# Seven products for eight of the sixteen expert tiles in six token-block pairs of a Fourier-mixing and expert-retrieval kernel, with operand sums formed on GpSimd

## The chip, the cores and the metric

The kernel runs on one core of a Trainium2 chip. The metric is the device time of one execution in microseconds (us). A core has five engines that run their own instruction streams in order and wait for each other by semaphores: TensorE (PE in the profile, with PEld for its weight loads), VectorE (DVE), ScalarE (ACT), GpSimd (POOL) and SyncE (SP), which issues the transfers here.

## What is computed

The input is 2048 tokens of 512 numbers, normalised first (`xn`). The result is the sum of three: the input, a Fourier mixing of `xn` by DFT matrices, and a retrieval of experts. The last takes nearly all the time:

```python
def _B_ref(x, w_q, k1, k2, u, v):            # H = 32 heads, E = 64, N = 4096 experts, K = 2
    q = jnp.einsum("nd,dhc->nhc", xf, w_q)
    s1 = jnp.einsum("nhd,ed->nhe", q[..., :dk], k1)
    s2 = jnp.einsum("nhd,ed->nhe", q[..., dk:], k2)
    ...
    top_s = jnp.take_along_axis(cand, ord2, axis=-1)
    top_e = jnp.take_along_axis(eidx, ord2, axis=-1)
    g = _softmax(top_s, axis=-1)
    ue = u[top_e]
    ve = v[top_e]
    act = _gelu(jnp.einsum("nd,nhkd->nhk", xf, ue))
    return jnp.einsum("nhk,nhk,nhkd->nd", g, act, ve)
```

Each token scores 64 + 64 half keys in each of 32 heads, keeps the two best of their sums, and adds up two experts of 4096 a head, weighted.

## The kernel before

**Numbers in two halves.** A float32 operand is kept as two float16 arrays, `h` (the rounded value) and `l` (the rest). A product is three matmuls, (h,h), (h,l) and (l,h), accumulated in PSUM. The split of a raw array is an ACT copy to `h` and a GpSimd subtraction for `l`.

**The scores.** The 32 heads are eight chunks j, the tokens 16 blocks i of 128. For each (j, i), 128 in all, `scores` (with `s_mm`) runs 12 matmuls of 512 columns (L247) into one of four PSUM banks, ACT evicts it (L891), and DVE finds the best values and their places (MAX8 L895, FIND_INDEX8 L899). M(j), the weights of a chunk, are products of the query weights and the keys: raw weights are split by ACT and GpSimd (`m_prep`; GpSimd's are L161 and L162) during the chunk before, and multiplied on PE (`m_mul`, L143) at fixed places amid the scores of that chunk, after i = 3, 4, 5 and 7. Routing of chunk j-1 (`routing`) is done by GpSimd and DVE in turns during chunk j, after i = 1, 2 and 4; the values to be combined pass between the two engines (L824 to L864). L535 and L536 fold rows of the Fourier part.

**Weights of the experts.** The 4096 experts are 16 tiles of 256, each two chunks of 128. `u` and `v` are loaded in float32, scaled and split by `fill_uv` and `stage_v` (ACT L774, L775 and L789; GpSimd L776 and L791) in slots of the table `todo`, a list of functions for each (j, i). `u` stays in SBUF; seven tiles of `v` go to the scratch `v_d` in DRAM. The list `fills` gives the order, u first for tiles 0 to 3, 8 to 14.

**The expert stage.** Instead of gathering, the kernel computes all activations of all experts and multiplies them with a sparse weight matrix. Phase z of a pair of token blocks (b, b+1) multiplies the two x blocks with all 32 chunks of u: `u_part` runs 12 matmuls of 256 columns for each chunk (L1027; two chunks to a bank), and ACT applies the gelu (L1034). Single blocks, 0, 1, 14 and 15, run with 128 columns. Then come two v phases, in which 96 matmuls of 512 columns (L1110) form the output of a block, and DVE and SP add and store it. In between the gates are built: one-hot matrices by DVE (L1055, L1060, L1063), multiplied on PE with 32 columns (L1065), and combined with the activations by DVE and ACT (L1073 to L1081). The order of phases is z0, z1, v0, then z(b,b+1), v(b-1), v(b) for b = 2, 4 to 12, then z14, v13, z15, v14, v15. Checks of the inputs' form run beside it (transfers named `cx` and `fit`), and if one fails, a slower version (`safe`) does the work again.

**What sets the order.** The program is written in a loop order with the tables `todo` and `plan`; a scheduler then arranges the instructions on each engine, which runs them in that order. A tile that is written again waits for all earlier readers, a store among them.

## Time and profile before

| | |
|---|---|
| median of 3 runs | 1146.23 us (1145.19 to 1146.46) |
| the profiled execution | 1147.81 us |
| its span | 1146.0 us |
| mean granted clock of TensorE | 0.996 |
| transfers over the span | 142.69 MB read, 17.63 MB written |

The span lies inside the execution's time. A window row names a stretch of the span and gives the time for which each engine was busy in it, with the count of its instructions in brackets, then the granted clock, the share of the 16 DMA engines, and GB/s. A group row names line, engine, operation and tiles, then a count; behind the bar it has the busy time, the mean of one in ns, and the idle time of the engine just before, with what ended it. A timeline row has the start, the duration and the line, and in brackets the idle time before it with the releaser. A piece of the chain of waits has a start, a duration and a count of instructions.

### The profile page before, as it was taken

To read this page: it belongs to the slowest core of one execution; us is meant where nothing else is said; L and a number is where in the kernel's file an instruction comes from. 1 tells how busy PE (TensorE), PEld (TensorE's weight loads), DVE (VectorE), ACT (ScalarE), POOL (GpSimd) and SP (SyncE) were. 2 spreads that over 40 slices of the span, in tenths; PEclk is the share of its full clock that TensorE was granted. 3 is DMA by queue.
4 is the path that set the end of the run, shared out by engine and by line. 5 is a ranking of instruction groups with operands and counts; after the bars stand their busy time and mean duration, and the time that the engine had idled before them with its cause. 6 is when DMAs were issued, how large, how long until landed. Compare 5 with 4: busy or idle time off the path is not lost.

```text
span 1146.0 us, 25270 instructions
## 1 busy us (share of the span) xinstructions
PE 1134.4 (99%) x9884; PEld 726.5 (63%) x9884; DVE 929.8 (81%) x2819; ACT 600.7 (52%) x1047; POOL 247.2 (22%) x265
## 2 busy tenths in 40 slices
PE   9999999999999999999999999999999999999997
PEld 6455454544544469687488478479569569658763
DVE  7899959899899999956985895896896796888570
ACT  6557487677686554353445445435526536433440
POOL 1415296675674400000000000000010010000000
PEclk8999999999999999999999999999999999999999
DMA  8884435234232104352742742742644545451422
GB/s 285 273 217 155 164 122 178 98 125 148 93 111 79 52 15 142 113 172 86 240 165 77 255 157 88 237 165 101 215 161 147 179 166 170 157 174 68 130 74 105
DMA packets 98335, 167.82 MB, mean 146 GB/s; under 512 B 32916, under 2 KB 48155, under 8 KB 98206
## 3 DMA queue, kind: packets, MB, share of 16 engines
q1 hardware_dynamic: 97904, 166.04, 43.1%
q8 instruction: 79, 1.29, 0.4%
q14 instruction: 50, 0.41, 0.1%
q10 hardware_dynamic: 302, 0.08, 0.0%
HBM read 142.69 MB, written 17.63 MB: 140 GB/s over the span
## 4 chain that ended last, share of the span: by engine, by line
PE 78%; DVE 12%; POOL 4%; DMA 2%; ACT 1%; issue 1%; SPq 0%; DVEq 0%; POOLq 0%; ACTq 0%
PE v L1110 28%; PE z L1027 27%; PE s L247 16%; PE g L1065 4%; DVE vals L895 3%; DVE idx L899 2%; PE m L143 1%; PE m L147 1%; DVE u L895 1%; POOL w L161 1%; DVE L L1055 1%; PE p L444 1%; DVE u L899 1%; DMA u<-in_vn_dram 1%; DVE act L1081 1%
## 5 line engine op out<-in xcount | busy, mean ns | idle before, releaser
L1027 PE MATMUL z<-xb,u 128*128 128x256 f16 (+1 forms) x3840 | 342.8, 251 | 0.1
L1027 PEld LDWEIGHTS <-u 128*128 128x128 f16 x3840 | 309.8, 98 | 26.5 <-issue 0.2
L247 PE MATMUL s<-m,xq 128*128 128x512 f16 x1344 | 297.2, 379 | 0.0
L1110 PE MATMUL v<-v,act 128*128 128x512 f16 x1056 | 233.2, 379 | 0.0
L247 PEld LDWEIGHTS <-xq 128*128 128x128 f16 x1344 | 129.7, 98 | 150.9 <-issue 1.0
L1055 DVE TENSOR_TENSOR L<-io_lam,cmp 128x2048 f16<-128x2048 f16 x128 | 156.1, 1220 | 60.4 <-PE g L1065 60.2
L1110 PEld LDWEIGHTS <-act 128*128 128x128 f16 x1056 | 101.4, 98 | 117.6
L1123 POOL TENSOR_TENSOR y<-y,xr 128x512 f32<-128x512 f32 x15 | 27.9, 1859 | 610.0 <-DMA y<-y_d 410.7
L895 DVE MAX8 vals<-ss 128x8 f32<-128x64 f32 x896 | 133.7, 216 | 6.3 <-ACT ss L891 6.2
L1034 ACT ACTIVATE act<-z,scl 128x256 f32<-128x256 f32 (+1 forms) x152 | 72.6, 502 | 121.7 <-PE z L1027 121.7
L1110 PE MATMUL v<-v,w 128*128 128x512 f16 x480 | 106.2, 379 | 0.0
L1186 ACT ACTIVATE cx<-cx 128x896 f32<-128x896 f32 x64 | 60.5, 945 | 69.7 <-DVE cx L1166 51.9
L891 ACT ACTIVATE ss<-s,wsc 128x512 f32<-128x512 f32 x120 | 79.4, 681 | 32.6 <-PE s L247 17.4
L899 DVE FIND_INDEX8 idx<-vals,ss 128x8 uint16<-128x256 f32 x224 | 93.9, 419 | 0.0
L1080 ACT ACTIVATE act<-w 128x1024 f16<-128x1024 f32 x36 | 48.4, 1360 | 62.6 <-DVE w L1073 62.1
L1110 PEld LDWEIGHTS <-w 128*128 128x128 f16 x480 | 46.1, 98 | 53.4
L1073 DVE SCALAR_TENSOR_TENSOR w<-act,scl,g 128x1024 f32<-128x1024 f32 x44 | 55.7, 1276 | 19.8 <-ACT act L1034 19.8
L1160 DVE TENSOR_TENSOR cx<-cx 128x512 f32<-128x512 f32 (+2 forms) x84 | 48.5, 612 | 26.8 <-DMA cx<-in_cb_dram 23.8
L1065 PEld LDWEIGHTS <-L 128*128 128x128 f16 x2048 | 60.7, 96 | 11.8 <-issue 1.3
L1081 DVE TENSOR_TENSOR act<-w,act 128x1024 f16<-128x1024 f32 x44 | 60.2, 1371 | 3.7 <-ACT act L1080 3.7
L1065 PE MATMUL g<-R,L 128*128 128x32 f16 x2048 | 61.9, 176 | 0.8 <-DVE R L1063 0.7
L1063 DVE TENSOR_TENSOR R<-R,cmp 128x512 f16<-128x512 f16 x128 | 60.8, 475 | 1.5
(320 smaller groups left out, 1318.5 us busy)
## 6 DMA issues: line engine op xcount, KB each, us to landing
v<-v_d SPq DMA_DIRECT2D x67, 512.0 KB, 4.1
cx<-in_cb_dram SPq DMA_DIRECT2D x64, 448.0 KB, 4.4
w<-in_wq_dram SPq DMA_DIRECT2D x28, 512.0 KB, 6.0
fit<-in_wq_dram SPq DMA_DIRECT2D x28, 512.0 KB, 5.0
uv<-in_vn_dram SPq DMA_DIRECT2D x16, 512.0 KB, 4.1
uv<-in_ut_dram SPq DMA_DIRECT2D x16, 512.0 KB, 5.7
c<-in_ca_dram SPq DMA_DIRECT2D x8, 512.0 KB, 7.2
y<-y_d SPq DMA_DIRECT2D x16, 256.0 KB, 3.6
```

The lines of the kernel that those rows point to most:

```text
L247: nc.tensor.matmul(ps, xt[i][:, l, kd, :], m[:, r, kd, :], start=(n == 0), stop=(n == 3 * KD - 1))
L891: nc.scalar.activation(s, ps, AF.Copy, scale=inv)
L895: nc.vector.max(vals[:, i, w, :, h], s[:, g, :])
L899: nc.vector.max_index(idx[:, i, w].rearrange("p k h -> p (k h)"), vals[:, i, w, 0:2].rearrange("p k h -> p (k h)"), s[:, w * HC:g + 1, :]. ...
L1027: nc.tensor.matmul(ps if n == 1 else ps.rearrange("p (b n) -> p b n", b=2), ug[:, l, c % 2, kd, :], xb2[:, k0, r, kd, :] if n == 1 else xb ...
L1034: nc.scalar.activation(ACT[bb][:, cg * m:cg * m + m, :], pv[:, i], AF.Gelu_apprx_tanh, scale=zsc)
L1055: nc.vector.tensor_tensor(L.rearrange("p t (l two) -> p t l two", two=2), io_lam.rearrange("p (l two) -> p l two", two=2).unsqueeze(1).to_ ...
L1063: nc.vector.tensor_tensor(Rv, Rv, bc(2, NC), op=ALU.mult)
L1065: nc.tensor.matmul(p[:, hf, t * NC:(t + 1) * NC], L[:, t, :], R[:, t, :], start=True, stop=True)
L1081: nc.vector.tensor_tensor(w16[..., 1], w, w16[..., 0], op=ALU.subtract)
L1110: nc.tensor.matmul(pv, w16[:, c, :, l], v_sb[g][:, r, cc, :], start=(n + cc == 0 and k == 0), stop=(n == 15 and cc == 1 and k == 2))
L1186: later.append(lambda: nc.scalar.activation(tf[:, P:], tf[:, P:], AF.Abs, accum_out=chk[:, n:n + 1]))
```

## The change

For the six pairs b = 2, 4 to 12, the eight tiles of the two quads (0 to 3) and (8 to 11) are multiplied in Winograd's form of Strassen's scheme: the two chunks of a tile, the two halves of the 512 long contraction and the two token blocks make a 2x2 by 2x2 block product, done with seven block products and additions. The other eight tiles, `PLAIN`, stay as they were.

- **Sums of u.** `sum_u` forms four sums of quarter tiles by GpSimd (L808 to L811 of the changed kernel), `split4` splits them (ACT L794, GpSimd L795) and stores both halves, 256 KB each, to the scratch `s_d`. It hangs behind `fill_uv` of the eight tiles.
- **Sums of x.** `sum_x` adds the halves of x (L821), forms four sums (L826 to L829), splits, and stores to `t_d`, once a pair, written at slots 62 + 7n. Both use the space of the v tiles 5 to 8 as scratch, which is filled later.
- **The products.** `z_pair` runs the products of both quads with the plain groups between them in the order of `SEQ`; `slot` is one product of 24 matmuls of 128 columns (L1153). Its weights are u itself or a tile of sums from a ring of three places (`ring_load`, L1136), its moving operand x or `x4`, the sums of the pair. A quad is three PSUM banks, X, Y and Z, that take several products each; ACT copies them out, DVE adds three times, and four gelus of 128x512 take the place of eight of 128x256.
- **PSUM.** Four banks `z0` to `z3` go round by a list (`take`, `banks`) in the expert stage; before, two tags had two buffers each.

```diff
+QUADS = (0, 1, 2, 3), (8, 9, 10, 11)
+PAIRS = tuple(range(2, 14, 2))
...
             nc.gpsimd.tensor_tensor(dl, raw, dh, op=ALU.subtract)
+            if which == 0 and not safe and any(g in q for q in QUADS):
+                SRAW[g] = raw
+                sum_u(g, 0)
+
+        def scratch(g):
+            return v_sb[g].rearrange("p l c d -> p (l c d)").bitcast(F32)
+
+        def split4(part, t, h, dst):
+
+            l = t.bitcast(F16)[:, 0:2 * D]
+            if part == 0:
+                nc.scalar.activation(h, t, AF.Copy)
+                nc.gpsimd.tensor_tensor(l, t, h, op=ALU.subtract)
+                return
+            for i, v in enumerate((h, l)):
+                nc.sync.dma_start(dst(i), v)
+
+        def sum_u(g, part):
+
+            qd, t = next((n, q.index(g)) for n, q in enumerate(QUADS) if g in q)
+            s4 = scratch(8)
+            if part == 0:
+                raw = SRAW.pop(g)
+                a = [raw[:, c, k * 256:k * 256 + 256] for c in range(2) for k in range(2)]
+                r = [s4[:, k * 256:k * 256 + 256] for k in range(4)]
+                nc.gpsimd.tensor_tensor(r[0], a[2], a[3], op=ALU.add)
+                nc.gpsimd.tensor_tensor(r[1], r[0], a[0], op=ALU.subtract)
+                nc.gpsimd.tensor_tensor(r[2], a[0], a[2], op=ALU.subtract)
+                nc.gpsimd.tensor_tensor(r[3], a[1], r[1], op=ALU.subtract)
+                return
+            split4(part - 1, s4, v_sb[6].rearrange("p l c d -> p (l c d)")[:, 0:2 * D],
+                   lambda i: s_d[qd].rearrange("o p (t l f) -> t l p o f", t=4, l=2)[t, i])
+
+        def sum_x(b, part):
+
+            f, t4 = scratch(5), scratch(7)
+            if part == 0:
+                v = xq[b // 2]
+                nc.gpsimd.tensor_tensor(f.rearrange("p (q f) -> p q f", q=2),
+                                        v[:, :, 0].rearrange("p q k n -> p q (k n)"),
+                                        v[:, :, 1].rearrange("p q k n -> p q (k n)"), op=ALU.add)
...
+                nc.gpsimd.tensor_tensor(r[0], b12, b11, op=ALU.subtract)
+                nc.gpsimd.tensor_tensor(r[1], b22, r[0], op=ALU.subtract)
+                nc.gpsimd.tensor_tensor(r[2], b22, b12, op=ALU.subtract)
+                nc.gpsimd.tensor_tensor(r[3], b21, r[1], op=ALU.subtract)
+                return
+            split4(part - 1, t4, v_sb[6].rearrange("p l c d -> p (l c d)")[:, 2 * D:],
+                   lambda i: t_d[b // 2, :, i * 2 * D:i * 2 * D + 2 * D])
...
+            if which == 0 and not safe and any(g in q for q in QUADS):
+                todo[n + 1].append(lambda at, g=g: (sum_u(g, 1), sum_u(g, 2)))
+        if not safe:
+            for n, b in enumerate(PAIRS):
+                for part, at in enumerate((0, 2, 3)):
+                    todo[62 + 7 * n + at].append(lambda at, b=b, part=part: sum_x(b, part))
...
-            p = (pc if (n == 2 or b == (0,)) and cg % 4 > 1 else pb)(f"z{b[0]}_{cg}")
+            p, tag = take(f"z{b[0]}_{cg}")
+            banks.append(tag)
...
+            SEQ = ["c", "1a", "2a", "5a", "c", "6a", "3a", "c", "7a", "c", "4a", "1b", "2b", "5b", "c", "6b", "3b", "c",
+                   "7b", "c", "4b", "c"]
...
+        def ring_load(at):
+            for p, (qd, o) in PENDING.pop(at, ()):
+                t = RING[qd, o] = sx.tile([P, 4, 2, 2, P], F16, tag=f"s{p}", name=f"s{qd}_{o}_{at}")
+                nc.sync.dma_start(t.rearrange("p t l k e -> p (t l k e)"), s_d[qd, o])
...
+        def slot(op, quad, bank, qd):
+
+            ua, us, ub, xa = OPS[op]
+            for t, g in enumerate(quad):
+                k = 0
+                for kd in range(2):
+                    for l, r in ((0, 0), (0, 1), (1, 0)):
+                        if us is None:
+                            lt = u_sb[g][:, l, ua // 2, ua % 2 * 2 + kd, :]
+                        else:
+                            lt = RING[qd, us][:, t, l, kd, :]
+                        rt = xb2[:, (0, 0, 1, 1)[xa], r, xa % 2 * 2 + kd, :] if ub is None else x4[:, r, ub, kd, :]
+                        nc.tensor.matmul(bank[:, t * P:(t + 1) * P], lt, rt, start=(t == k == 0 and op in "125"),
+                                         stop=(t == 3 and k == 5), skip_group_check=op not in "125")
+                        k += 1
+            if us is not None:
+                ring_load(used[0])
+                used[0] += 1
...
+                    if op == "1":
+                        nc.scalar.activation(dst(0, 0), v(X), AF.Copy)
+                    elif op == "2":
+                        nc.vector.tensor_tensor(dst(0, 0), v(Y), dst(0, 0), op=ALU.add)
+                        banks.append(Yt)
+                    elif op == "5":
+                        nc.scalar.activation(dst(1, 0), v(Z), AF.Copy)
+                    elif op == "6":
+                        nc.scalar.activation(dst(0, 1), v(X), AF.Copy)
+                        gelu(dst(0, 0))
+                    elif op == "3":
+                        nc.vector.tensor_tensor(dst(0, 1), v(Z), dst(0, 1), op=ALU.add)
+                        banks.append(Zt)
+                    elif op == "7":
+                        nc.scalar.activation(dst(1, 1), v(X), AF.Copy)
+                        nc.vector.tensor_tensor(dst(1, 1), dst(1, 1), dst(1, 0), op=ALU.add)
+                        gelu(dst(0, 1))
+                    else:
+                        gelu(dst(1, 0), v(X))
+                        gelu(dst(1, 1))
+                        banks.append(Xt)
```

The lines of the changed kernel are numbered later: L535, L536 become L540, L541; L161, L162 become L166, L167; L776 and L791 become L782 and L849; L824 becomes L882.

**GpSimd at the end of chunk j=0 and in the first third of j=1**, up to the first row of routing. Here `u` in the folds are buffers of the Fourier part. Before:

```order
L535 TENSOR_TENSOR u_126<-u_126 128x127
L535 TENSOR_TENSOR u_126<-u_126 128x128
L536 TENSOR_TENSOR u_126<-u_126 128x127
L536 TENSOR_TENSOR u_126<-u_126 128x128
L824 TENSOR_TENSOR c_0_1304<-u_132 128x64
```

Now (v_920 and v_922 are the scratch of the sums, v_921 their upper halves, xq_108 the x of a pair):

```order
L795 TENSOR_TENSOR v_922<-v_922,v_921 128x1024
L828 TENSOR_TENSOR v_922<-v_920 128x256
L540 TENSOR_TENSOR u_128<-u_128 128x127
L540 TENSOR_TENSOR u_128<-u_128 128x128
L541 TENSOR_TENSOR u_128<-u_128 128x127
L541 TENSOR_TENSOR u_128<-u_128 128x128
L826 TENSOR_TENSOR v_922<-v_920 128x256
L827 TENSOR_TENSOR v_922<-v_920,v_922 128x256
L829 TENSOR_TENSOR v_922<-v_920,v_922 128x256
L821 TENSOR_TENSOR v_920<-xq_108 128x1024
L882 TENSOR_TENSOR c_0_1306<-u_134 128x64
```

The third pair's subtraction, the fourth pair's operations and the addition for the fifth now stand ahead of routing of j=0, behind the work for the first and second. The six sums of x as a whole moved to j=0 and j=1, and three subtractions L795 of theirs stand between this routing and the next weights' first split. L826 writes the place that the store behind L795 reads.

**GpSimd in chunk j=3**, from a split of an expert tile to the first row of routing (`w` are the next chunk's weights). Before:

```order
L776 TENSOR_TENSOR u_128<-uv_3_2341,u_128 128x1024
L161 TENSOR_SCALAR w_124<-w_124,wsc 128x1024
L162 TENSOR_TENSOR w_124<-w_124,wh_0_2477 128x1024
L776 TENSOR_TENSOR u_133<-uv_8_2418,u_133 128x1024
L161 TENSOR_SCALAR w_124<-w_124,wsc 128x1024
L162 TENSOR_TENSOR w_124<-w_124,wh_1_2536 128x1024
L824 TENSOR_TENSOR c_0_2622<-vals_1927 128x64
```

Now, from the first of those weights on:

```order
L166 TENSOR_SCALAR w_126<-w_126,wsc 128x1024
L167 TENSOR_TENSOR w_126<-w_126,wh_0_2507 128x1024
L795 TENSOR_TENSOR v_923<-v_923,v_921 128x1024
L782 TENSOR_TENSOR u_135<-uv_8_2444,u_135 128x1024
L810 TENSOR_TENSOR v_923<-uv_8_2444 128x256
L808 TENSOR_TENSOR v_923<-uv_8_2444 128x256
L809 TENSOR_TENSOR v_923<-v_923,uv_8_2444 128x256
L811 TENSOR_TENSOR v_923<-uv_8_2444,v_923 128x256
L166 TENSOR_SCALAR w_126<-w_126,wsc 128x1024
L167 TENSOR_TENSOR w_126<-w_126,wh_1_2574 128x1024
L795 TENSOR_TENSOR v_923<-v_923,v_921 128x1024
L882 TENSOR_TENSOR c_0_2664<-vals_1941 128x64
```

Two sums of four operations and a subtraction (of the tiles 3 and 8; the four operations of tile 3 stand just ahead of these rows) now lie between that split and routing. The same happens with the tiles 0 and 1 in j=2 and with 9, 10 and 11 in j=4.

**SP in the z phase of the pair (4, 5)**, the transfers of the checks and the ring. Before:

```order
L875 DMA_TRANSPOSE zt_9807<-z_d 128x3x128
L1122 DMA xr_9046<-in_x_dram 128x512
L1139 DMA cx_8199<-in_ca_dram 128x128
L1140 DMA cx_8199<-in_cb_dram 128x896
L1237 DMA fit_8233<-in_wq_dram 128x1024
L1139 DMA cx_8302<-in_ca_dram 128x128
```

Now:

```order
L933 DMA_TRANSPOSE zt_10418<-z_d 128x3x128
L1298 DMA xr_9499<-in_x_dram 128x512
L1136 DMA s_3_8_8333<-s_d 128x2048
L1315 DMA cx_8575<-in_ca_dram 128x128
L1316 DMA cx_8575<-in_cb_dram 128x896
L1136 DMA s_3_9_8430<-s_d 128x2048
L1413 DMA fit_8634<-in_wq_dram 128x1024
L1315 DMA cx_8729<-in_ca_dram 128x128
L1136 DMA s_0_11_8512<-s_d 128x2048
L1136 DMA s_1_10_8458<-s_d 128x2048
```

The ring's loads take their places among the checks'. Each waits until the product that read its place last has ended. s_3_9 is the operand of product 3 of the first quad; PE's order ahead of its first use is product 6, a plain group, product 7 (which the scheduler moved ahead of 3) and one matmul.

More of the change, by code (lines that the diff above doesn't have):

```diff
@@ L1306, in part_b, with take @@
         stP.close()
+        stQ.close()
+        psz = stE.enter_context(tc.tile_pool(name="psz", bufs=1, space=bass.MemoryType.PSUM))
+        banks = ["z0", "z1", "z2", "z3"]
+        def take(name):
+            tag = banks.pop(0)
+            return psz.tile([P, 512], F32, tag=tag, name=name), tag
         psg = stE.enter_context(tc.tile_pool(name="psg", bufs=1, space=bass.MemoryType.PSUM))
@@ L1385, in part_b, with after @@
                     ACT[c] = BT[c] if c < 2 else act_tile(c)
+                def after(cg):
+                    for f in plan.get((ph, cg), ()):
+                        f()
+                if not safe and b[0] in PAIRS and len(b) == 2:
+                    z_pair(b, PAIRS.index(b[0]), after)
+                    continue
                 for cg in range(8 * len(b)):
                     u_part(b, cg)
-                    for f in plan.get((ph, cg), ()):
-                        f()
+                    after(cg)
                 continue
             b = ph[1]
-            pv = pc(f"v{b}")
+            if b == 0:
+                ring_load(-1)
+            pv, pvt = take(f"v{b}")
             if phases[n + 1:n + 2] and phases[n + 1][0] == "z":
```

83 lines of the change are left out of this document (75 added, 8 removed).

## The prediction

> **What bounds the kernel now.** I read the page's head first, then its chain of waits, then busy times in stretches, and then the rows of GpSimd (POOL) that the change lengthens.
>
> ```profile
> span 1146.0 us, 25270 instructions
> PE 1134.4 (99%) x9884; PEld 726.5 (63%) x9884; DVE 929.8 (81%) x2819; ACT 600.7 (52%) x1047; POOL 247.2 (22%) x265
> PE 78%; DVE 12%; POOL 4%; DMA 2%; ACT 1%; issue 1%; SPq 0%; DVEq 0%; POOLq 0%; ACTq 0%
> ```
>
> TensorE (PE) is busy for 99% of the span, and most of the chain is its own work. GpSimd's 22% is an average that says nothing: nearly all of it lies in the score stage. The windows show this; the first four are the chunks j=1 to j=4 of the scores, the last is one token-block pair of the expert stage.
>
> ```profile
> core 0: us, PE busy (x) PEld busy (x) DVE busy (x) ACT busy (x) POOL busy (x), PEclk, DMA share, GB/s
> 105.00:154.60 49.60, 48.53 (x330) 26.46 (x329) 42.14 (x248) 34.84 (x79) 23.64 (x36) 1.00 0.36 126
> 154.60:199.20 44.60, 44.39 (x293) 22.23 (x292) 36.76 (x183) 34.59 (x61) 32.35 (x39) 1.00 0.47 168
> 199.20:243.50 44.30, 44.30 (x290) 21.62 (x289) 41.01 (x210) 33.01 (x48) 29.30 (x27) 1.00 0.34 120
> 243.50:287.70 44.20, 44.20 (x289) 21.52 (x288) 40.89 (x209) 32.96 (x48) 29.22 (x27) 1.00 0.34 120
> 668.30:758.00 89.70, 89.70 (x834) 62.73 (x833) 69.46 (x117) 42.00 (x78) 4.01 (x2) 1.00 0.49 167
> ```
>
> In a chunk of the scores GpSimd works 29 of 44 us, in order, and its 15 us of idle time are pieces between waits. In a pair PE has no idle time at all. So the change takes work from PE where PE is the bound, and hands it to GpSimd where GpSimd is nearly one.
>
> **The matmuls.** A pair has 32 chunks of 12 matmuls of 256 columns, 384 in all. Eight groups of 24 stay; the other 192 become 14 products of 24 matmuls of 128 columns, 336. The chain of waits inside one pair gives the price of the old form, the whole chain near the end, where single blocks run with 128 columns and a weight load for each, that of the new.
>
> ```profile
> 578.51 7.87 PE z L1027 x72
> 1045.00 5.37 PE z L1027 x96
> ```
>
> 7.87/72 is 109.3 ns and 5.37/96 is 55.9 ns. Before 192 × 109.3 ns = 20.98 us, after 336 × 55.9 ns = 18.78 us: 2.2 us less a pair, **−13.2 us** for six. Seven products for eight are an eighth less; the operation count promises no more than 2.6 us a pair, and the shorter form gives back a little.
>
> [...]
>
> **What the pairs get besides.** Per pair six 512 KB transfers are added: five operand tiles into a ring of three places, and the sums of x. A ring place is loaded again when the product that used it last is done.
>
> ```profile
> v<-v_d SPq DMA_DIRECT2D x67, 512.0 KB, 4.1
> L1127 DVE SCALAR_TENSOR_TENSOR y<-v,scl,y 128x512 f32<-128x512 f32 x16 | 11.9, 746 | 19.6 <-PE v L1110 19.6
> L891 ACT ACTIVATE ss<-s,wsc 128x512 f32<-128x512 f32 x120 | 79.4, 681 | 32.6 <-PE s L247 17.4
> ```
>
> A tile of that size lands 4.1 us after its issue. The operand of product 3 in the first quad is issued when 6 ends; PE then has a plain group and product 7 to do, 24 × 0.109 + 24 × 0.056 + 0.11 = 4.1 us. That of 7 in the second quad is issued when 3 ends, with a group and a bit of g ahead, 2.62 + 0.54 = 3.2 us. With a semaphore or two and the issue itself, 0.2 to 1 us each, PE waits some 0.4 and 1.2 us, 1.6 us a pair: **+9.6 us**. If the loads land early it is 0; if all five are late by 0.7 us it is 20. DVE gains six additions of 0.75 us a pair on 69 of 90 us, ACT eight copies of 0.68 us and the gelus in half as many, longer pieces, on 42 of 90: these hide behind PE. Four PSUM banks in rotation hold X, Y, Z and a plain group, and a bank comes free one gelu or one addition later than its matmuls, about 0.7 us against 1.3 or 2.6 us of the product that follows.
>
> **What GpSimd gets.** For each of eight expert tiles four operations of 128x256 and a subtraction of 128x1024, for each of six pairs an addition of 128x1024 besides.
>
> ```profile
> L162 POOL TENSOR_TENSOR w<-w,wh x24: 2122/2134/2141, 83.2 to 349.2; 128x1024 f16<-128x1024 f32 x24
> L844 POOL TENSOR_TENSOR if<-if,hoff x7: 613/613/614, 114.0 to 384.0; 128x256 f32<-128x256 f32 x7
> v_d<-vh SPq DMA_DIRECT2D x7, 256.0 KB, 4.4
> L774 ACT ACTIVATE u<-uv,ss 128x1024 f16<-128x1024 f32 x16 | 18.4, 1149 | 0.5
> ```
>
> An expert tile costs 4 × 0.61 + 2.13 = 4.57 us, a pair 6.70 us: 37 and 40 us, on an engine that has worked 247. Consecutive sums share their scratch: the first operation that writes it again waits until the store of the one before has landed, 4.4 us, and everything behind it on GpSimd waits too. Between a sum's last operation and its subtraction stands ACT's copy, 1.15 us.
>
> **j=1.** All six sums of x run in j=0 and j=1, ahead of and among routing. GpSimd before:
>
> ```profile
> 80.28 2.85 POOL L161 TENSOR_SCALAR w<-w,wsc 128x1024 f32<-128x1024 f32 x1 [24.57 <-ACT wh L157]
> 88.27 6.31 POOL L162 TENSOR_TENSOR w<-w,wh 128x1024 f16<-128x1024 f32 x3
> 102.53 0.88 POOL L535 TENSOR_TENSOR u<-u 128x127 f32<-128x127 f32 x2 [2.55 <-ACT u L532]
> 110.97 0.32 POOL L824 TENSOR_TENSOR c<-u 128x64 f32<-128x64 f32 x1 [1.63 <-DVE u L895]
> 119.41 0.32 POOL L835 TENSOR_TENSOR g<-c,g 128x64 f32<-128x64 f32 x1
> 142.94 2.85 POOL L161 TENSOR_SCALAR w<-w,wsc 128x1024 f32<-128x1024 f32 x1 [4.43 <-ACT wh L157]
> ```
>
> The first sum and the next addition fit into the 24.57 us of idle time. Then, in the new order: first subtraction to 90.4, splits to 97.4, three operations and an addition to 101.4, second subtraction to 103.5, two folds, the store lands at 107.9, third subtraction to 115.8, the next store lands at 120.2. Routing of j=0 begins at 124.1 in place of 110.97, 13 us late, and ends at 132.9. The last three subtractions end at 135.0, 145.5 and 155.0, each after a store, and the first split for the next weights begins after one more operation, at 157.2 in place of 142.94: **14.2 us late**.
>
> **j=2.** Two expert sums, 9.1 us, stand among these splits, up to the one that PE waits for.
>
> ```profile
> 169.80 4.22 POOL L162 TENSOR_TENSOR w<-w,wh 128x1024 f16<-128x1024 f32 x2
> 171.98 0.20 PE L143 MATMUL m<-sums,w 128*128 128x64 f16 x1 [0.21 <-POOL w L162]
> ```
>
> PE already waits 0.21 us there, so nothing covers a delay. GpSimd idles only about 1 us in pieces between 142.94 and 169.80. The price of j=1 and j=2 together is 14.2 + 9.1 − 1 = **22 us**. If all stores landed before they are asked for, 12.7 us of waits would fall away, and 9 would stay; if the copies queue behind evictions (0.68 us each, one or two at each of eight sums) and GpSimd waits for them, it is 30.
>
> **j=3.**
>
> ```profile
> 191.07 2.13 POOL L776 TENSOR_TENSOR u<-uv,u 128x1024 f16<-128x1024 f32 x1 [2.03 <-DMA v_d<-vh]
> 193.46 2.85 POOL L161 TENSOR_SCALAR w<-w,wsc 128x1024 f32<-128x1024 f32 x1 [0.26 <-ACT wh L157]
> 205.62 0.32 POOL L824 TENSOR_TENSOR c<-vals 128x64 f32<-128x64 f32 x1
> 210.65 2.13 POOL L162 TENSOR_TENSOR w<-w,wh 128x1024 f16<-128x1024 f32 x1
> 216.17 0.22 PE L143 MATMUL m<-sums,wh 128*128 128x64 f16 x2
> ```
>
> Two more sums, 9.1 us, come between 191 and routing; the second waits 4.4 − 2.13 − 0.61 = 1.7 us for a store. GpSimd has about 1.4 us of idle time there, and the split that ends at 212.78 is wanted at 216.17: 3.4 us of cover. 9.1 + 1.7 − 1.4 − 3.4 = **6 us** (3 to 8).
>
> **j=4.** Three sums, 13.7 us and 1.7 us for a store, on top of the 3.4 us of cover already used, against the idle pieces
>
> ```profile
> 225.12 2.14 POOL L776 TENSOR_TENSOR u<-uv,u 128x1024 f16<-128x1024 f32 x1 [4.80 <-ACT uv L775]
> 231.25 2.13 POOL L791 TENSOR_TENSOR uv<-uv,vh 128x1024 f16<-128x1024 f32 x1 [4.00 <-ACT uv L789]
> 235.43 2.13 POOL L776 TENSOR_TENSOR u<-uv,u 128x1024 f16<-128x1024 f32 x1 [2.05 <-ACT uv L775]
> ```
>
> that is 10.9 us, 1.4 us of small waits as in j=3 and the cover of 3.4 us: 18.8 − 15.7 = **3 us** (0 to 7). The sum of the tile that runs in j=3's first, idle third (two waits of 4 us) costs nothing.
>
> **Sum.** 1147.8 (the profiled execution) − 13.2 + 9.6 + 22 + 6 + 3 = 1175.2 us. The profiled execution is 1.6 us above the median of the runs shown, so I forecast **1174 us**. With all costs at their low ends (0 for the ring, 9 + 3 + 0 for GpSimd) it is 1145, at their high ends (20, 30 + 8 + 7) 1198.
>
> **Rivals.**
>
> *The sums hide.* If each store lands in time and GpSimd's 15 us of idle time a chunk take up the rest, only the matmuls and the ring are left: 1146.2 − 13.2 + 0 to 10, about 1133 to 1143, faster. For it speak the idle 24.57 us before j=1 and the 11 us in j=4; against it that PE waits for GpSimd already in j=2, where the added 9.1 us have no idle time to go to. It decides if the delay there stays under 3 us. 0.12.
>
> *GpSimd's longer work also holds up DVE and ACT.* DVE's small operations of routing stretch when GpSimd works beside them:
>
> ```profile
> 260.47 2.14 POOL L162 TENSOR_TENSOR w<-w,wh 128x1024 f16<-128x1024 f32 x1
> 260.55 2.14 DVE L836 CAST z<-g 128x128 f16<-128x128 f32 x1 [0.50 <-POOL g L835]
> L836 DVE CAST z<-g x9: 168/2132/2139, 122.9 to 433.4; 128x128 f16<-128x128 f32 x7, 128x32 f16<-128x32 f32 x1, 128x96 f16<-128x96 f32 x1
> ```
>
> The cast, 0.17 us in its shortest form, ends when GpSimd's subtraction does. With 76 us more of GpSimd, some ten more such operations at 2 us, and ACT's evictions behind copies that wait for GpSimd, add 20 to 30 us: about 1200. Against it: few of DVE's 210 operations of a chunk are of that kind, and while they wait PE still has the four PSUM banks of scores to fill. 0.16. [...]
>
> *Weight loads bound the short matmuls.* A load alone takes 98 ns:
>
> ```profile
> L1027 PEld LDWEIGHTS <-u 128*128 128x128 f16 x3840 | 309.8, 98 | 26.5 <-issue 0.2
> ```
>
> If each of 336 paid that instead of 55.9 ns, it would be 32.9 us a pair, 12 more than now: +71 in place of −13, about 1260. Against it stand the 96 at 55.9 ns. [...] 0.02.
>
> *The gain is eaten and nothing else happens.* The ring costs 13 us, GpSimd nothing: 1146. 0.03. That the sums don't run where the change puts them is a fact of the new order: it has the sums of x two chunks earlier than their slots say, which is what makes j=1 dear.
>
> **How the numbers follow.** My forecast has 0.67. A difference under 0.2% (2.3 us) can't be told from no change by such a measurement. Faster: 0.12 and 0.02 from the low end of the forecast's case, 0.14. Same: 0.03. Slower: the rest, 0.83. The range for 8 in 10 is 1143 to 1203: below, the forecast's low end and the edge of the first rival, above, the second rival's centre and a little.
>
> **What would show it.** In the changed profile's windows PE has idle time in j=1, j=2 and j=3, with GpSimd named as releaser of the m matmuls and of DVE's routing, and its operations of 128x256 wait for stores; the experts' stage starts some 31 us later than now; a pair takes about 89.1 us in place of 89.7, with two short waits of PE for s_d. The prediction is wrong if the expert stage starts within 5 us of where it did, if the 128-column products take over 60 ns a matmul, or if a pair loses more than 4 us to loads or to PSUM banks.

## The result and the profile after

The changed kernel takes 1215.24 us (median of 6 runs, 1208.81 to 1218.84) against 1145.62: a ratio of 1.0604 (95% interval 1.0573 to 1.0634). It is 69.6 us slower. The forecast was 28 us slower, 1174 us, and its range ended at 1203: the sign was right, the time lies outside. The page's head and the shares of the chain, changed kernel:

```profile
span 1214.2 us, 27275 instructions
PE 1142.1 (94%) x10748; PEld 731.7 (60%) x10748; DVE 949.1 (78%) x2855; ACT 631.6 (52%) x1061; POOL 328.2 (27%) x341
PE 59%; POOL 13%; DVE 13%; DMA 6%; ACT 5%; issue 3%; SPq 0%; POOLq 0%; ACTq 0%
```

GpSimd has 81 us more work, 4 more than reckoned (37 + 40). But PE's share of the chain fell from 78% to 59%, while GpSimd's rose from 4% to 13%, that of transfers from 2% to 6% and ScalarE's from 1% to 5%. The windows are cut at the first matmul of each chunk of the scores; the last row goes from the last score to the end. First the kernel before, then the changed one, each with j=0 to j=4 and the rest:

```profile
23.90:103.70 79.80, 78.95 (x369) 42.29 (x369) 75.07 (x267) 47.92 (x98) 31.10 (x32) 1.00 0.81 244
103.70:153.70 50.00, 48.93 (x332) 26.64 (x330) 43.29 (x253) 34.72 (x78) 23.29 (x38) 1.00 0.35 121
153.70:199.20 45.50, 45.29 (x298) 22.64 (x297) 36.91 (x183) 35.49 (x63) 33.25 (x39) 1.00 0.48 169
199.20:243.50 44.30, 44.30 (x290) 21.62 (x289) 41.01 (x210) 33.01 (x48) 29.30 (x27) 1.00 0.34 120
243.50:287.70 44.20, 44.20 (x289) 21.52 (x288) 40.89 (x209) 32.96 (x48) 29.22 (x27) 1.00 0.34 120
417.50:1146.00 728.50, 721.40 (x7426) 512.65 (x7424) 554.88 (x1012) 316.80 (x559) 29.06 (x17) 1.00 0.44 148
```

```profile
23.50:108.40 84.90, 79.13 (x368) 42.33 (x368) 75.37 (x264) 46.89 (x93) 42.98 (x38) 0.99 0.79 238
108.40:180.10 71.70, 53.61 (x330) 28.30 (x330) 43.09 (x243) 36.25 (x80) 50.75 (x65) 0.84 0.33 107
180.10:240.50 60.40, 50.36 (x298) 24.31 (x297) 39.99 (x197) 40.39 (x73) 51.70 (x60) 0.89 0.54 170
240.50:299.90 59.40, 50.03 (x289) 22.76 (x288) 39.41 (x197) 34.51 (x51) 46.94 (x46) 0.91 0.38 112
299.90:348.00 48.10, 44.91 (x289) 21.70 (x289) 40.33 (x205) 35.52 (x52) 33.05 (x29) 1.00 0.39 131
479.80:1214.20 734.40, 712.08 (x8290) 513.63 (x8288) 571.21 (x1048) 336.41 (x559) 29.05 (x17) 1.00 0.53 174
```

Nearly all of it is in the scores: they end 62 us later (479.8 in place of 417.5 us), and the expert stage is 5.9 us longer. Two things add up in j=0 to j=4. PE stands still: the length of a window less PE's busy time in it gives 5.8 + 18.1 + 10.0 + 9.4 + 3.2 = 46.5 us, against 2.1 before. And PE's own work takes longer: 198.9 us busy in j=1 to j=4, against 182.7 for the same matmuls. The granted clock of j=1 to j=3 is 0.84 to 0.91, a mean that counts the time in which PE stands still (a window of e8, below, has 0.50 with 44 of its 48 us a wait). What PE waits for over the whole span: first, in the kernel before, its wait for a small scale that ScalarE makes, then the three longest of the changed kernel (total us, times, longest):

```profile
PE m L143 <- ACT uvpFalse L117: 1.1, 1, 1.1
```

```profile
PE s L252 <- ACT ss L949: 22.6, 16, 5.5
PE m L148 <- ACT uvpFalse L122: 17.6, 1, 17.6
PE z L1153 <- DMA s<-s_d: 14.6, 10, 3.7
```

To these come 5.7 us for GpSimd's weight splits, the way on which the prediction had put all of j=2 to j=4. Most waits go to ScalarE: for evictions (L949) and for that scale (L122). GpSimd, then ScalarE, then PE in j=1 show why:

```profile
118.34 2.13 POOL L795 TENSOR_TENSOR v<-v,v 128x1024 f16<-128x1024 f32 x1
133.09 0.72 POOL L826 TENSOR_TENSOR v<-v 128x256 f32<-128x256 f32 x1 [10.14 <-DMA t_d<-v]
137.56 0.32 POOL L882 TENSOR_TENSOR c<-u 128x64 f32<-128x64 f32 x1
```

```profile
140.45 0.26 ACT L890 ACTIVATE c<-c 128x64 f32<-128x64 f32 x1 [12.77 <-POOL c L887]
140.61 0.67 ACT L949 ACTIVATE ss<-s,wsc 128x512 f32<-128x512 f32 x1
141.18 0.16 ACT L122 ACTIVATE uvpFalse<-uvs 128x2 f32<-128x2 f32 x1
```

```profile
141.39 0.27 PE L148 MATMUL m<-sums,wh 128*128 128x64 f16 x2 [17.62 <-ACT uvpFalse L122]
```

The subtraction of the third sum of x ends at 120.47; the store behind it lands 12.6 us later, where 4.4 was assumed: SyncE issued its second half at 125.4, after a wait of 5.8 us that the profile puts down to an eviction of ScalarE, and that half took 7.55 us. Routing of j=0 begins at 137.56 (110.97 before, 124.1 predicted). ScalarE's exponential of that routing stands in its queue ahead of evictions and of a small scale (L122) that PE's weight products need, so PE stands still for 17.6 us, 12.8 of them while ScalarE waits. In j=2 to j=4 the copies of the sums (L794) do the same; first two of them, then the matmuls behind them, with one score from the start of j=1 ahead:

```profile
199.68 1.06 ACT L794 ACTIVATE v<-v 128x1024 f16<-128x1024 f32 x1 [5.44 <-POOL v L811]
273.55 1.06 ACT L794 ACTIVATE v<-v 128x1024 f16<-128x1024 f32 x1 [6.84 <-POOL v L811]
```

```profile
108.44 5.28 PE L252 MATMUL s<-m,xb 128*128 128x512 f16 x12 [4.96 <-ACT ss L949]
202.40 4.59 PE L252 MATMUL s<-m,xq 128*128 128x512 f16 x12 [5.52 <-ACT ss L949]
275.24 8.29 PE L252 MATMUL s<-m,xq 128*128 128x512 f16 x24 [2.84 <-ACT ss L949]
```

Each copy waits for GpSimd's four operations, behind it wait the evictions, and for them PE. The wait of 4.96 us at the start of j=1 is of the same kind: a copy for a sum of x had waited 12.44 us. These PE rows also show slow matmuls: 12 of a score take 2.59 us in the kernel before, at a granted clock of 1.00, here 5.28 us right after a wait of 4.96 us.

In the expert stage the products did nearly what was reckoned. Two pairs of the changed kernel:

```profile
712.90:803.00 90.10, 87.84 (x977) 62.70 (x976) 71.75 (x115) 44.61 (x79) 3.90 (x2) 1.00 0.61 202
984.50:1072.20 87.70, 87.68 (x977) 62.70 (x976) 72.95 (x122) 45.25 (x81) 3.99 (x2) 1.00 0.57 194
```

PE is busy for 87.7 to 88.1 us of each of the last five pairs in place of 89.7 to 89.8, and the last one, which has no wait for `s_d`, lasts 87.7; the others lose the gain to such waits. In the first pair PE is busy as long as before (66.7 us in the same part of it, at a granted clock of 0.98), so that all six together save 9.2 us.

### The profile page after: what moved, and what is told of

Read it like the earlier page. It is cut to its first block, busy times and chain, and to the rows that moved or that the text cites. A ratio compares the mean times of both kernels' runs of the same rounds, so it can differ in the third digit from the quotient of the medians.

```text
span 1214.2 us, 27275 instructions
## 1 busy us (share of the span) xinstructions
PE 1142.1 (94%) x10748; PEld 731.7 (60%) x10748; DVE 949.1 (78%) x2855; ACT 631.6 (52%) x1061; POOL 328.2 (27%) x341
## 4 chain that ended last, share of the span: by engine, by line
PE 59%; POOL 13%; DVE 13%; DMA 6%; ACT 5%; issue 3%; SPq 0%; POOLq 0%; ACTq 0%
PE v L1286 26%; PE z L1092 14%; PE z L1153 8%; PE s L252 4%; DVE vals L953 4%; PE g L1241 4%; DMA s<-s_d 3%; DVE idx L957 3%; PE p L449 2%; POOL w L167 2%; POOL w L166 2%; POOL u L782 2%; PE m L152 1%; POOL v L795 1%; DMA t_d<-v 1%
## 5 line engine op out<-in xcount | busy, mean ns | idle before, releaser
L252 PE MATMUL s<-m,xq 128*128 128x512 f16 x1344 | 308.9, 388 | 15.6 <-ACT ss L949 15.6
L252 PEld LDWEIGHTS <-xq 128*128 128x128 f16 x1344 | 132.3, 100 | 176.1 <-issue 33.0
L1092 PE MATMUL z<-xb,u 128*128 128x128 f16 (+1 forms) x2688 | 222.8, 243 | 0.0
L1092 PEld LDWEIGHTS <-u 128*128 128x128 f16 x2688 | 196.9, 98 | 13.3 <-issue 0.2
L1362 ACT ACTIVATE cx<-cx 128x896 f32<-128x896 f32 x64 | 60.5, 945 | 66.8 <-DVE cx L1342 48.6
L949 ACT ACTIVATE ss<-s,wsc 128x512 f32<-128x512 f32 x120 | 78.3, 676 | 13.5 <-DVE idx L957 8.8
L1099 ACT ACTIVATE act<-z,scl 128x256 f32<-128x256 f32 (+1 forms) x88 | 44.2, 524 | 74.4 <-PE z L1092 74.4
L1256 ACT ACTIVATE act<-w 128x1024 f16<-128x1024 f32 x36 | 48.3, 1357 | 60.4 <-DVE w L1249 60.0
L1153 PEld LDWEIGHTS <-s 128*128 128x128 f16 x1080 | 61.9, 98 | 16.6 <-DMA s<-s_d 16.4
L1336 DVE TENSOR_TENSOR cx<-cx 128x512 f32<-128x512 f32 (+2 forms) x84 | 48.6, 610 | 28.6 <-DMA cx<-in_cb_dram 28.6
L1241 PEld LDWEIGHTS <-L 128*128 128x128 f16 x2048 | 61.2, 96 | 11.5 <-DVE R L1239 1.2
L1249 DVE SCALAR_TENSOR_TENSOR w<-act,scl,g 128x1024 f32<-128x1024 f32 x44 | 55.9, 1280 | 11.1 <-ACT act L1099 11.1
L1257 DVE TENSOR_TENSOR act<-w,act 128x1024 f16<-128x1024 f32 x44 | 60.4, 1377 | 3.7 <-ACT act L1256 3.7
```

The costliest lines, as they stand in the source:

```text
L252: nc.tensor.matmul(ps, xt[i][:, l, kd, :], m[:, r, kd, :], start=(n == 0), stop=(n == 3 * KD - 1))
L949: nc.scalar.activation(s, ps, AF.Copy, scale=inv)
L1092: nc.tensor.matmul(ps if n == 1 else ps.rearrange("p (b n) -> p b n", b=2), ug[:, l, c % 2, kd, :], xb2[:, k0, r, kd, :] if n == 1 else xb ...
L1153: nc.tensor.matmul(bank[:, t * P:(t + 1) * P], lt, rt, start=(t == k == 0 and op in "125"), stop=(t == 3 and k == 5), skip_group_check=op ...
L1241: nc.tensor.matmul(p[:, hf, t * NC:(t + 1) * NC], L[:, t, :], R[:, t, :], start=True, stop=True)
L1249: nc.vector.scalar_tensor_tensor(w, act[:, :, ts], fw, p.rearrange("p h (n c) -> p c (h n)", c=NC), op0=ALU.mult, op1=ALU.mult)
```

## The experiments

The table has what all the runs but the one on the clock (e8) rest on: the time from one chunk's first matmul to the next one's, and from the last score to the end of the span, in the profiled execution of each, then the median of all its executions (us). The kernel before had medians of 1145.6 to 1147.9 beside these runs.

| kernel | j=0 | j=1 | j=2 | j=3 | j=4 | j=5 to 7 | rest | median |
|---|---|---|---|---|---|---|---|---|
| before | 79.8 | 50.0 | 45.5 | 44.3 | 44.2 | 129.8 | 728.5 | 1145.6 |
| changed | 84.9 | 71.7 | 60.4 | 59.4 | 48.1 | 131.8 | 734.4 | 1215.2 |
| e1 no sums | 79.8 | 50.0 | 45.5 | 44.2 | 44.3 | 129.8 | 737.4 | 1153.8 |
| e2 sums alone | 84.9 | 71.9 | 58.9 | 60.8 | 48.1 | 131.9 | 727.8 | 1209.7 |
| e3 copies on GpSimd | 79.8 | 81.9 | 59.0 | 52.3 | 53.6 | 131.9 | 736.7 | 1216.7 |
| e4 own scratch | 99.9 | 63.2 | 57.5 | 59.2 | 48.1 | 130.7 | 733.3 | 1217.2 |
| e5 sums of x late | 79.8 | 50.0 | 57.1 | 60.4 | 47.6 | 132.2 | 750.6 | 1202.3 |
| e13 copies held | 80.6 | 50.1 | 55.1 | 48.7 | 49.0 | 131.8 | 753.3 | 1190.5 |
| e14 spread, not held | 79.8 | 50.0 | 45.5 | 49.5 | 51.4 | 143.9 | 747.1 | 1194.4 |
| e6 spread and held | 79.7 | 50.1 | 45.5 | 44.2 | 44.2 | 132.8 | 750.5 | 1175.6 |
| e7 as e6, ring of four | 79.8 | 50.1 | 45.5 | 44.2 | 44.2 | 134.0 | 765.5 | 1191.2 |
| e9 all placed | 80.2 | 50.0 | 49.0 | 44.3 | 45.0 | 134.9 | 749.3 | 1174.7 |
| e10 as e9, ring rule 2 | 80.0 | 50.2 | 49.0 | 44.2 | 45.1 | 134.8 | 741.3 | 1171.1 |
| e11 as e9, ring rule 3 | 79.8 | 50.0 | 50.7 | 44.2 | 44.2 | 134.6 | 738.8 | 1170.2 |
| e12 sums of x on VectorE | 79.8 | 50.2 | 45.5 | 44.2 | 44.2 | 133.9 | 729.4 | 1153.8 |

**The parts alone.** e1 forms no sums and stores halves of u and x in their place:

```diff
-                SRAW[g] = raw
-                sum_u(g, 0)
+                pass
...
-            for i, v in enumerate((h, l)):
+            for i, v in enumerate((h, h)):
```

> The operand sums are left out: GpSimd forms none of them and ScalarE copies none; the stores to s_d and t_d and all products of the expert stage stay (halves of u and x are stored in place of the sums). Theory S (all 62 us of the score stage come from the sums on GpSimd and the copies behind them): the scores end where they did before (417.5 us, within 3), the expert stage takes 734 us as in the changed kernel, time 1149 to 1156. Rival T (stores, queue and PSUM banks have a share of more than 10 us): 1165 or more.

e2 forms the sums and runs the old z phase:

```diff
-                if not safe and b[0] in PAIRS and len(b) == 2:
+                if False:
                     z_pair(b, PAIRS.index(b[0]), after)
```

> All sums are formed, split and stored, but the expert stage runs the 384 matmuls of 256 columns as before and loads no sums. Theory S: the scores end at 480 us as in the changed kernel, the expert stage takes 728 us, time 1205 to 1213. Rival T: under 1195.

1153.8 and 1209.7 us: theory S on both counts. The stores cost the scores nothing; the sums on GpSimd and ScalarE cost all of the 62 us. And with sums for nothing the kernel would still be a little slower than before, 1.0046 (1.0025 to 1.0068), for PE waits in e1's expert stage as in the changed kernel's:

```profile
PE z L1152 <- DMA s<-s_d: 15.3, 10, 4.6
```

**Who copies, and where the scratch lies.** e3:

```diff
-                nc.scalar.activation(h, t, AF.Copy)
+                nc.gpsimd.tensor_copy(h, t)
```

> The 14 copies to float16 of the sums run on GpSimd in place of ScalarE. Theory A (evictions of scores stand on ScalarE behind copies that wait for GpSimd, and PE's banks run out): PE's waits for evictions fall from 22.6 us to under 8 and the time to 1185 to 1205, although GpSimd has 14 more instructions of 1 to 2 us. Rival B (GpSimd's lateness itself is the cost, whoever copies): its 15 to 30 us more come on top, 1225 to 1245.

e4 (the places of `h` in turn likewise):

```diff
-            s4 = scratch(8)
+            s4 = scratch((8, 4)[m % 2])
...
-            f, t4 = scratch(5), scratch(7)
+            f, t4 = scratch(5), scratch((7, 0, 1)[m])
```

> The sums of x take turns in three places of scratch and those of u in two, so that no sum waits for the store of the one just before. Theory C (waits for stores on GpSimd, 10.1 + 2.1 + 1.6 us in j=1, make routing of j=0 late): j=1 shortens by 10 to 20 us and the time falls to 1190 to 1205. Rival (ScalarE's copies or GpSimd's own work decide): 1208 to 1220, routing as late as before.

1216.7 and 1217.2 us, no change: theories A and C fell, and B too; the rival beside C held. In e3 no copy of a sum stands on ScalarE, but its exponential waits for routing longer than ever:

```profile
145.51 0.26 ACT L890 ACTIVATE c<-c 128x64 f32<-128x64 f32 x1 [28.60 <-POOL c L887]
210.68 0.26 ACT L890 ACTIVATE c<-c 128x64 f32<-128x64 f32 x1 [18.20 <-POOL c L887]
```

PE stands still for 30.1 us at the first of these, and its waits for evictions stay at 21.3 us, most of them now behind the exponentials of j=2 to j=4. In e4 no sum waits for a store in j=1, but the scheduler now put more of the sums ahead of routing, which begins at 140.46, and two copies in j=0 waited 14.0 and 10.3 us for GpSimd, with PE idle for 19.0. In both the five chunks together are within 4 us of the changed kernel's 324.5. Taking one wait away moved the loss to the next: what was late was GpSimd.

**Place.** e5 forms the sums of x in the expert stage, from the x blocks loaded for the next pair:

```diff
-                    nc.sync.dma_start(x4.rearrange("p l o k n -> p (l o k n)"), t_d[phases[n + 1][1] // 2])
+                    sum_x(phases[n + 1][1])
```

> The sums of x are formed in the expert stage, from the x blocks loaded for the next pair during the v phase ahead of it, and go straight to x4; the sums of u stay as in the changed kernel. Theory P (GpSimd's total work and waits between one routing and the next set the score stage, whoever copies and wherever the scratch lies; what the sums of x put ahead of routing in j=1 costs there): j=0 and j=1 as before (79.8 and 50.0 us), j=2 to j=4 still 30 to 40 us over the 134 before, time 1185 to 1197. Rival Q (the sums of u carry the loss, those of x only shift it): above 1205.

j=0 and j=1 are as before to 0.1 us, so the sums of x cost 26.8 us there; the sums of u cost 31.1 us in j=2 to j=4 (165.1 against 134.0). Theory P, but the time is above its range, since the expert stage became 16 us longer than the changed kernel's. Next, e6 is e5 with three things more: it fills the quads' tiles two to a chunk right behind routing, holds the copies back, and gives the sums of u two places of scratch in turn:

```diff
-QUADS = (0, 1, 2, 3), (8, 9, 10, 11)
+QUADS = (4, 5, 6, 7), (8, 9, 10, 11)
...
+            fills = [(0, g) for g in (0, 1, 2, 3, 12, 8, 9, 13, 14, 10, 11, 15)] + [
+                (1, 0), (0, 4), (0, 5), (1, 1), (1, 2), (0, 6), (0, 7), (1, 3), (1, 4)] + [(1, g) for g in range(5, V2)]
...
-                todo[n + 1].append(lambda at, g=g: (sum_u(g, 1), sum_u(g, 2)))
+                todo[n + 3].append(lambda at, g=g: (sum_u(g, 1, at), sum_u(g, 2)))
...
-                nc.scalar.activation(h, t, AF.Copy)
+                nc.scalar.activation(h, t, AF.Copy, scale=behind(one, at))
```

(`behind` writes the scale in the row of a score's eviction, so the copy can't stand ahead of it.)

> As the run with late sums of x; besides, the quads are tiles 4 to 7 and 8 to 11, filled two to a chunk in j=3 to j=6 right behind routing, where GpSimd waited 10.9 us for ScalarE; each sum has its own scratch in turn, and its copy on ScalarE is held back three score blocks. The work is the same as in the changed kernel. Theory P: the scores end within 6 us of 417.5, time 1150 to 1160, like the kernel without sums (1153.8). Rival R (any 43 us more on GpSimd cost PE most of that, wherever they stand): 1180 or more.

The scores end at 420.5 us, 3.0 later than before, with the same 41 us of sums of u on GpSimd: theory P. The time, 1175.6, is again above its range, since the expert stage takes 750.5 us. e13 and e14 tell apart what e6 changed at once: e13 is e5 with the last two edits and scratch in turn, e14 is e6 without the last two edits.

> As the run with late sums of x (score stage 35 us over the kernel before), only that ScalarE's copy of each sum of u is held back three score blocks and two places of scratch are taken in turn; the tiles and their slots are those of the change. Theory H (evictions behind copies that wait): j=2 to j=4 take under 150 us in place of 165. Theory P (GpSimd's place ahead of splits and routing): 158 to 168 us.

> As the run with spread sums of u, only that the copies on ScalarE are not held back. Theory P: the scores end within 8 us of 417.5 again. Theory H: ScalarE's copies wait for GpSimd as in the change, PE waits for evictions 15 us or more in j=3 to j=6, and the scores end at 435 or later.

PE's waits in e13, then in e14:

```profile
PE m L148 <- POOL w L167: 11.1, 3, 7.3
PE s L252 <- ACT ss L932: 4.6, 5, 2.2
```

```profile
PE s L252 <- ACT ss L932: 18.5, 10, 3.4
```

Held copies without better places take j=2 to j=4 from 31.1 to 18.8 us over the kernel before; most of what is left is waits for GpSimd's splits. (Scratch in turn came with them; in e4, without held copies, j=2 to j=4 were 3 us shorter than in the changed kernel.) Better places without held copies leave 26.6 us over in j=3 to j=6: 18.5 us of waits for evictions, and slow matmuls behind them. Each of the seven waits of more than 1 us follows a copy that had itself waited 4.5 to 6.9 us for GpSimd. Both theories have a share, but the shares don't add: of the 31 us of e5 holding alone takes off 12, placing alone 5, and both together 28.

**The clock.** e8 is the kernel before with nothing added but a wait:

```diff
+        def stall(at):
+            t = behind(M[5][1], at)
+            for n in range(5):
+                d = dram.tile([P, 1], F32, name=f"ch{n}")
+                nc.sync.dma_start(d, t)
+                t = cst.tile([P, 1], F32, name=f"cs{n}")
+                nc.sync.dma_start(t, d)
+            M[5] = M[5][0], t
```

> The kernel before, with a chain of ten small transfers in chunk j=5 that the scale of its last eight evictions waits for; no engine has more work, PE only stands still for some 10 to 20 us. Theory K (PE's clock is lower for some us after it stood still): PE's busy time in j=5 rises by 3 us or more over the 44.3 before, and the granted clock there falls under 0.95. Rival (the lower clock of the changed kernel comes from the work on GpSimd and ScalarE): PE's busy time stays at 44.3 and the clock at 1.00.

```profile
368.68 12.18 PE L247 MATMUL s<-m,xq 128*128 128x512 f16 x48 [48.60 <-ACT ss L891]
```

The wait came out longer than meant. The 48 matmuls behind it took 12.18 us in place of 10.36, and j=5 had 46.1 us of busy time against 44.3: 1.8 us more, not the 3 expected. The granted clock in windows, first e8 from within the wait to 3.4 us past its end, then two of the changed kernel at the waits of 4.96 and 2.08 us:

```profile
324.27:372.06 47.79, 3.38 (x9) 1.19 (x9) 3.40 (x24) 4.12 (x7) 0.00 (x0) 0.50 0.02 2
```

```profile
107.17:113.99 6.82, 5.55 (x15) 2.39 (x15) 5.57 (x36) 3.59 (x14) 6.58 (x10) 0.50 0.21 77
250.53:253.94 3.41, 3.40 (x9) 1.17 (x9) 2.02 (x12) 3.41 (x5) 3.33 (x3) 0.50 0.62 212
```

So a stall alone, without more work on any engine, is followed by slow matmuls at a granted clock of 0.50, as theory K says, but the price did not grow with the stall's length. In the changed kernel's trace 60 of the scores' matmuls behind six stalls of 2.08 to 17.62 us start over 260 ns after the one before, most of them 426 to 428 ns in place of 216; they come 6 to 14 in a run and cost 1.2 to 2.9 us each time, the least behind the longest stall, 12.2 us in all of the 16.2. A wait of 2.08 us was enough once; no wait of up to 1.85 us in j=2 to j=4 was followed by half the clock. What sets the clock back was not shown.

**The ring and the expert stage.** e7 is e6 with a fourth place, taken from the buffers `w`:

```diff
-        WB = 4
+        WB = 3
...
-                    free = [p for p in range(3) if p not in held]
+                    free = [p for p in range(4) if p not in held]
```

> As the run with spread sums of u, with four places in the ring in place of three (the room is taken from one of the four buffers w). Four of eight operand tiles are then loaded a pair, each some 10 us ahead of its use. Theory L (PE's 15 us of waits for s_d and the slow clock behind them eat the gain of the products): the waits for s_d fall under 2 us and the time to 1132 to 1142, faster than before. Rival M (the room taken from w, or DVE and ScalarE, hold the pairs): 1148 or more.

1191.2 us. The waits for `s_d` were gone, but PE waited 25.9 us for the one-hot rows R of VectorE in place of 13.3 in e6: rival M. On the ring alone this gives no verdict, since a buffer of `w` was taken with it. e9 keeps the ring as it was and puts the sums of x back into the scores, into GpSimd's idle time:

```diff
-                for part, at in enumerate((0, 2, 3)):
-                    todo[62 + 7 * n + at].append(lambda at, b=b, part=part: sum_x(b, part))
+            for n, b in zip((22, 25, 40, 120, 121, 122), PAIRS):
+                todo[n].append(lambda at, b=b: sum_x(b, 0, at))
+                todo[n + 3].append(lambda at, b=b: (sum_x(b, 1, at), sum_x(b, 2)))
```

> All the work of the changed kernel, placed elsewhere: sums of u as in the run with spread sums; the sums of x in the scores again, each held back to a slot where GpSimd waited before (two in j=1 and one in j=2 behind routing, three in the second half of j=7), with scratch of its own, and its copy on ScalarE three score blocks later. Theory P (place, not amount): the scores end within 8 us of 417.5 and the expert stage takes 734 to 738 us again, since GpSimd is idle there; time 1152 to 1164. Rival R (amount): 1175 or more.

The chunks take 9.8 us more than before, less than a sixth of the change's 62, with all its work. But the expert stage, expected at 734 to 738 us, took 749.3: the last sums came so late that the first gelu stood behind their copies, the last of which waited 5.3 us for GpSimd.

```profile
PE z L1107 <- ACT act L1114: 8.8, 1, 8.8
```

So the time, 1174.7 us, is above P's range and all but in R's, though the scores came out as P has it. e10 and e11 are e9 with another rule for the place that is given up (2 and 3 products back):

```diff
-                        p = max(far, key=lambda p: (far[p], -last[p]))
+                        ok = [p for p in far if last[p] <= n - 2] or [min(far, key=lambda p: last[p])]
+                        p = max(ok, key=lambda p: (far[p], -last[p]))
```

> As the run with all sums placed, with another rule for the ring of three places: a place is given up only if its last use lies two products back, so a load has at least one product more to land; 38 loads in all in place of 33. Theory L (waits for s_d and the slow clock behind them eat the products' gain): PE's waits for s_d fall from 15 us to under 6 and the time by 8 to 14 us against the same kernel with the old rule, near the 1146 of the kernel before. Rival M (more transfers collide with those of v and the checks): no change or slower.

> As the run before it, with three products back: 48 loads, each with two products more to land. Theory L: waits for s_d under 2 us, time 1138 to 1148, 10 to 18 us below the same kernel with the old rule. Rival M (48 loads of 512 KB, 8 MB more, slow the transfers of v and the checks): slower than the rule with two products back.

1171.1 and 1170.2 us, 3.6 and 4.6 below e9: the direction of theory L and less than half its size, with runs of one kernel up to 10 us apart, so that a gain in time is not shown. PE's waits for `s_d` fell from 16.1 to 10.5 and to none, but in e11 it waits 9.4 us for ScalarE's copies of the products, in place of 1.5. A pair of e11 takes 87.8 to 89.9 us:

```profile
757.40:845.20 87.80, 87.65 (x977) 62.70 (x976) 76.87 (x147) 45.99 (x83) 3.72 (x2) 1.00 0.67 227
```

e12 is e6 with e11's rule for the ring, and it forms the sums of x on VectorE (`nc.vector` for `nc.gpsimd` in e5's `sum_x`).

> As the run with spread sums of u (scores 3 us longer than before), with the rule of three products back for the ring, and with the sums of x for the next pair formed by DVE in place of GpSimd in the v phase. Theory N (GpSimd's 45 us in the expert stage held up DVE's one-hot operations, and the ring's loads held up PE; without both the products gain 6 to 13 us): time 1138 to 1146, expert stage 716 to 724 us. Rival O (DVE, 69 us busy of 90, has no room for 27 us more in six pairs, or ScalarE's copies bind): 1149 or more.

1153.8 us, 1.0058 (1.0040 to 1.0077): rival O. The expert stage is back at 729.4 us, 21 less than in e6, but PE still waits 5.8 us for ScalarE's copies of the products and 4.9 for VectorE. Of the versions that form all sums it is the fastest, 61 us below the change, yet not faster than the kernel before; none tried was.

## Why the prediction was wrong

- **What bounds, and the sign: right.** Work left PE, which was the bound, for GpSimd, which was nearly one; e1 and e2 show that all of the scores' loss is the sums'.
- **Products, −13.2 us: the right price, a smaller gain.** 96 of the 128-column matmuls take 5.36 us (55.8 ns each), PE is busy 1.6 to 2.1 us less in five of the pairs (2.2 predicted), and a pair without waits lasts 87.7 us. The first pair gained nothing, and the six together 9.2 us. The rival with loads as the bound of short matmuls fell.
- **Ring, +9.6 us: under-sized.** 14.6 us of waits. The 0.2 to 1 us for semaphores and the issue was the author's estimate; in the changed kernel the issue of a load takes 0.33 us and the load lands 4.2 us after it begins (medians; 3.3 to 6.8 to landing). The expert stage came out 9.5 us over the forecast of 3.6 less.
- **j=1, 14.2 us: GpSimd's lateness foreseen, the path not.** The loss is 26.8 us with j=0. Routing was late by 26.6 us and not 13. In this trace one store, which landed after 12.6 us, has 8 of that; 4.4 was taken from the profile of before for every store, as if SyncE had nothing else to issue. But in e4, without such waits, routing began no earlier. And the prediction had PE wait for the next weights' splits; in j=1 it waited 17.6 us for the scale behind ScalarE's exponential, and for no split.
- **j=2 to j=4, 17 us: the step that failed.** 33.9 us. The prediction let GpSimd's lateness reach PE only through the weight splits, gave each of ScalarE's copies 1.15 us and at most one or two evictions, and held that PE's four banks cover such waits. In the trace copies stood 3 to 9 us at the head of ScalarE's queue until GpSimd was done, and PE waited 13.4 us for evictions behind five of them, against 5.7 us for splits. In e13, with the copies held back, 18.8 us remain of e5's 31.1. That this is close to the 17 is in part luck, since only 11.1 us of it are waits for splits and the slow matmuls, which the prediction left out, are in it.
- **The clock: a missing term.** The sum reckoned a stall at its length. PE's matmuls took 16 us longer in j=1 to j=4, 11.5 of these in j=2 to j=4; e8 shows that a stall alone does this, 1.8 us there.
- **GpSimd's prices.** Four operations of 128x256 take 2.9 to 3.0 us, not 2.44: another 7 us over 14 sums, if each instruction is counted by itself.

```profile
81.18 0.73 POOL L826 TENSOR_TENSOR v<-v 128x256 f32<-128x256 f32 x1
84.16 2.13 POOL L821 TENSOR_TENSOR v<-xq 128x1024 f32<-128x1024 f16 x1
```

Of the rivals, the second (evictions behind waiting copies, 1200 us, 0.16) named half of the missing mechanism and set it aside because of the four banks. Its other half, routing's operations on VectorE stretched by GpSimd, did not show in the scores: VectorE is busy there for 361.9 us, before for 358.9. The first rival, that the sums hide, did not come true with these places, but e6 shows that in the scores they can.

## What to carry to other kernels

Idle time of an engine is worth only what lies where the work can go: the same 41 us of sums of u cost 31 us ahead of what others wait for (e5), and 3 us behind it with their copies held back (e6). If work is handed to a side engine, price every instruction on other engines that must wait for it by what stands behind it in its own queue, here the evictions that feed the bound engine, and hold it back until its input is ready. And add a price for each stall of PE besides its length, here 1.2 to 2.9 us for each of six stalls of 2.08 us and more.

## What was not expected of the hardware

A single stall of 48.6 us cost 1.8 us of slow matmuls (e8), and in the changed kernel five stalls of 2.1 to 5.5 us cost 1.6 to 2.9 us each. A 256 KB store that shared SyncE's queue with others landed 12.6 us after its data were ready, 7.55 us of that after its issue; in the kernel before, the stores `v_d<-vh` of that size landed 4.4 us after their issue in the median, those of `y_d` 7.1.

What slowed the expert stage by 16 us with GpSimd's sums in it (e5 and e6, against the changed kernel) is settled in part. PE waited there 12.7 and 13.3 us for R, against 0.4. VectorE was busy for 588.5 us of e6's expert stage, against 571.2, and its multiplication for R took 509 ns in place of 454:

```profile
L1239 DVE TENSOR_TENSOR R<-R,cmp 128x512 f16<-128x512 f16 x128 | 58.1, 454 | 1.3
L1236 DVE TENSOR_TENSOR R<-R,cmp 128x512 f16<-128x512 f16 x128 | 65.1, 509 | 1.3
```

(The changed kernel, then e6.) So VectorE took longer for the same work in the run with the sums on GpSimd; with the sums on VectorE itself (e12) the multiplication took 470 ns, and in the kernel before, without sums, 475. The sums also shared the buffers `w` with VectorE's work, in e12 too, and no run separates the two.
